# A recurrent attention block in front of a mixture of experts: the recurrence in halves of 64 steps, with matrix products of 64x64

## The chip, the core and the metric

The kernel runs on one core of one Trainium2 chip. Its time is the device time of one execution in microseconds (us); the time before is the median of three runs. A core has five engines that run their own instruction streams and wait for each other by semaphores: TensorE (PE in the profile, with its weight loads as PEld), VectorE (DVE), ScalarE (ACT), GpSimd (POOL) and SyncE (SP), which here issues most of the DMAs.

## What is computed

```python
# r, k, v: (4, 8, 768, 48); w, u: (8, 48); all fp32
for t in range(S):
    cur = np.einsum('bhd,bhe->bhde', u[None] * kt, vt)
    y[:, :, t] = np.einsum('bhd,bhde->bhe', rt, state + cur)
    state = w[None, :, :, None] * state + np.einsum('bhd,bhe->bhde', kt, vt)
# x: y as (3072 tokens, 384); then a mixture of experts, 4 groups of 4
g_idx = argmax(x @ w_group);  e_idx = argmax(x @ w_expert[g_idx])
out[token] = g_w * e_w * (relu(x @ w1[g, e]) @ w2[g, e])     # w1: 384x1024, w2: 1024x384
```

The gates `g_w` and `e_w` are the softmax values at the two chosen places. Each token goes to one expert of 16.

## The kernel before

**Tiles of the recurrence.** The 768 steps of each of the 4 sequences are cut into 6 chunks of 128. A tile `n` is one chunk of one sequence: `c = n // 4`, `b = n % 4`, 24 tiles, each with all 8 heads. Heads go in pairs: `hc` is the pair (4 of them), `e` the head in it, and a head is padded from 48 to 64 so that a pair fills 128 partitions. Decay is not applied step by step: r and k are scaled by powers of w (`T1T`, `T2`) that run over three chunks (`SPAN`), and the state is multiplied by the decay of the whole span (`w_span`) after each third chunk.

**One tile, in order.** `turn` transposes r and the scaled k of a tile on TensorE into two PSUM banks (`pr`, `pk`); VectorE scales `pr` into `rT`, ScalarE copies `pk` into `kT`. `scores` multiplies k and r of a tile, per head a product of 128 keys with 128 queries over 48 rows, into `pa0` and `pa1`; VectorE masks them by `later` into `am`. `values` adds the earlier state's share (`R`, one 128x128 product per pair, with zeros off the two diagonal blocks) and the products of `am` and v into one bank `py`; ScalarE copies it into `yT`. It then computes the update k times v into `pu`, and VectorE adds it to the state, for each half of the partitions on its own. `back` transposes `yT` into `pb`, and VectorE adds the step's own term `dv` into the token rows `xt`. `own` (GpSimd), `own_sum` (VectorE) and `own_values` (ScalarE, eight multiplications) make that term. `rows_T` transposes the rows again (`px`, copied by ScalarE to `xT`), and `row_logits` multiplies them by the gate weights into a bank `rb`.

**Routing.** After each four tiles the tokens are given to experts: `choice` (13 small VectorE operations and one exponential on ScalarE), `before` (two matrix products into a bank `pre`, which count the tokens ahead of each), `gate` and `place` (VectorE; `place` reads `pre`), and `rows`, an indirect DMA on GpSimd's queue that scatters the rows into `x_sorted`. `zero_places` fills the beginnings of the 16 regions of `x_sorted` with zeros, by DMAs on ScalarE's queue.

**The order** is written out by hand: every engine runs its instructions in the order of the program (line 103). The loop at line 691 goes over steps `s`: in step `s` the tile `s` is turned, `scores` runs for tile `s-1`, `values` for `s-2`, `back` for `s-3`, `rows_T` for `s-4`, `row_logits` for `s-5`. A step issues in this order: `before`; `turn`; GpSimd's scaling and `own`; `own_values`; `choice`; `rows_T`; `row_logits`; `back`; `values`; `own_sum`; `gate`, `place` and `rows`; `scores`. Choice runs in steps 9, 13, 17, 21 and 25, and `before`, `gate` and `place` in the step after each.

**Buffers.** PSUM has eight banks. Six form one set (line 82) that every user takes from as banks come free, and two are kept for routing (line 84). A bank is free again when its last reader has run. r and k are held in rings of four pairs of tiles, v in one of five. The weights of every second expert are later loaded into the memory of these rings.

**Experts.** From step 26 on the experts are computed, one item after another: `columns` (rows transposed into `px`), `up` (`ph`), `down` (`po`), `rows_out` (`pb`). The two largest experts' weights are loaded in steps 23 and 25, as soon as four chunks have been counted.

Of the kernel before, what the change touches and what calls it, by code (L numbers as in the profile page):

```python
# [30 lines left out]
RING = 4  # L31
# [3 lines left out]
def kernel(  # L35
# [29 lines left out]
    assert RING * 2 * H * D == KO * F and RING * 2 * H * DP >= FO * DM  # L65
# [16 lines left out]
    psum = ctx.enter_context(tc.tile_pool(name="psum", bufs=6, space=bass.MemoryType.PSUM))  # L82

    rpsum = ctx.enter_context(tc.tile_pool(name="rpsum", bufs=2, space=bass.MemoryType.PSUM))

    def bank(shape, name):
        return psum.tile(shape, FP32, tag="bank", name=name)
# [24 lines left out]


# [4 lines left out]
    khs = ring([P, 2, H, DP], "kh", RING - 1)  # L118
# [41 lines left out]

    first_use = cst([P, 1], "first_use")
# [16 lines left out]
    R = ring([P, HP, P], "R", B)  # L178
# [22 lines left out]
    for t in R:  # L201
        nc.gpsimd.memset(t, 0.0)
# [118 lines left out]
    def zero_places(j):  # L321

        regions = xs_dram.rearrange("(e n) w -> n e w", e=GE)
        part = CAP // 4
        nc.scalar.dma_start(out=regions[part * j : part * (j + 1)], in_=spread(nothing[0:part, :], 1, GE))
# [3 lines left out]
    def route_bank():  # L329

        return rpsum.tile([P, 512], FP32, tag="route", name="rb")

    def route(pool, rb, xt, T, sums, number, group):
# [28 lines left out]
        def choice():  # L362
            nc.vector.reduce_max(out=mx, in_=L, axis=AX)

            nc.vector.tensor_tensor(out=key, in0=L, in1=spread(mx, 3, Eg), op=OP.is_ge)
            nc.vector.tensor_mul(
                key.rearrange("p i a e -> p (i a) e"), key.rearrange("p i a e -> p (i a) e"), spread(desc, 1, T * NA)
            )
            nc.vector.reduce_max(out=kx, in_=key, axis=AX)
            nc.vector.tensor_tensor(out=ohg, in0=key[:, :, 0, :], in1=spread(kx[:, :, 0], 2, Eg), op=OP.is_equal)  # L370
            nc.vector.tensor_tensor(out=ohx, in0=key[:, :, 1:NA, :], in1=spread(kx[:, :, 1:NA], 3, Eg), op=OP.is_equal)
            nc.vector.tensor_mul(ohe, ohx, spread(ohg, 3, Eg))
            nc.vector.tensor_mul(ohp, ohx, spread(ohg, 3, Eg))
            for i in range(T):
                nc.vector.tensor_add(sums[:, i + 1, :], sums[:, i, :], ohp[:, i].rearrange("p g e -> p (g e)"))
            nc.vector.tensor_sub(ex, L, spread(mx, 3, Eg))
            nc.scalar.activation(ex, ex, AF.Exp)
# [30 lines left out]
        def rows(i):  # L408
# [8 lines left out]
        return choice, before, gate, place, rows  # L417
# [4 lines left out]
            kall.rearrange("p j a h d -> p (j a h d)").rearrange("p (k f) -> p k f", f=F),  # L422
# [53 lines left out]
    def columns(i):  # L476
        xg, w = xgs.pop(i), width(i)
        xe = xes[i] = item_tile(i, [P, KO, room(i)], "xe")
        for ks in (range(0, KO),) if KO * w <= 512 else (range(0, 2), range(2, KO)):
            px = bank([P, len(ks), w], "px")  # L480
            for q, ko in enumerate(ks):
                for j, n in enumerate(parts(i)):
                    nc.tensor.transpose(  # L483
                        px[:, q, P * j : P * j + n], xg[0:n, j, P * ko : P * (ko + 1)], ident[0:n, 0:n]
                    )
            nc.vector.tensor_copy(xe[:, ks[0] : ks[-1] + 1, 0:w], px)  # L486
        ids = item_tile(i, [P, 2], "ids", U32, bufs=4)
        gates = item_tile(i, [P, 2], "gates", bufs=4)
        for j, n in enumerate(parts(i)):
            nc.vector.tensor_scalar(  # L490
                out=ids[0:n, j : j + 1], in0=xg[0:n, j, DM + ROW_ID : DM + ROW_ID + 1], scalar1=float(N),
                scalar2=None, op0=OP.add,
            )
            nc.vector.tensor_copy(gates[0:n, j : j + 1], xg[0:n, j, DM + ROW_GATE : DM + ROW_GATE + 1])
        keys_of[i] = ids, gates

    def up(i, f):

        w = width(i)
        if f == 0:  # L500
            hTs[i] = item_tile(i, [P, FO, room(i)], "hT")
        w1, xe = weights[ITEMS[i][0]][0], xes[i]
        ph = bank([P, 2, w], "ph")
        for q in range(2):
            for ko in range(KO):
                nc.tensor.matmul(  # L506
                    ph[:, q, :], lhsT=w1[:, ko, P * (f + q) : P * (f + q + 1)], rhs=xe[:, ko, 0:w],
                    start=(ko == 0), stop=(ko == KO - 1), skip_group_check=True,
                )
        nc.scalar.activation(hTs[i][:, f : f + 2, 0:w], ph, AF.Relu)  # L510

    def down(i, d):

        w = width(i)
        if d == 0:
            yo[i] = item_tile(i, [P, KO, room(i)], "yo")
        w2, hT = weights[ITEMS[i][0]][1], hTs[i]
        po = bank([P, w], "po")
        for fo in range(FO):
            nc.tensor.matmul(  # L520
                po, lhsT=w2[:, fo, P * d : P * (d + 1)], rhs=hT[:, fo, 0:w], start=(fo == 0), stop=(fo == FO - 1)
            )
        nc.scalar.copy(yo[i][:, d, 0:w], po)  # L523

    def rows_out(i):
        y, (ids, gates) = yo.pop(i), keys_of.pop(i)
        for j, n in enumerate(parts(i)):
            pb = bank([P, DM], "pb")
# [17 lines left out]
    def scale_k(g, engine, a0=0, a1=2):  # L546
        m = g // (B // 2) % SPAN
        engine.tensor_mul(khs[g % (RING - 1)][:, a0:a1, :, 0:D], kts[g % RING][:, a0:a1], spread(T2[m], 1, a1 - a0))  # L548
# [20 lines left out]
    def turn(n):  # L569
# [3 lines left out]
        for dst, src in ((pr, rts[g % RING]), (pk, khs[g % (RING - 1)])):  # L573
# [7 lines left out]

    def scores(n):
        kT, rT = rkT[n]
        am = ams[n] = pool.tile([P, 2, HP, P], FP32, tag="am", bufs=2, name="am")
        pa = [bank([P, HP, P], f"pa{e}") for e in range(2)]
        for hc in range(HP):
            for e in range(2):
                rows = slice(DP * e, DP * e + D)
                nc.tensor.matmul(  # L589
                    pa[e][:, hc, :], lhsT=kT[rows, hc, :], rhs=rT[rows, hc, :],  # L590
                    start=True, stop=True, skip_group_check=True,
                )
        for e in range(2):
            nc.vector.tensor_mul(am[:, e], pa[e], spread(later, 1, HP))  # L594

    def values(n):
# [3 lines left out]
        vt, kh = vts[g % (RING + 1)], khs[g % (RING - 1)]  # L600
        rT, am = rkT.pop(n)[1], ams.pop(n)
        py = bank([P, HP, P], "py")
        if c > 0:
            for hc in range(HP):
                nc.tensor.matmul(
                    py[:, hc, :], lhsT=R[b][:, hc, :], rhs=rT[:, hc, :], start=(hc == 0), stop=False,
                    skip_group_check=True,
                )
        for hc in range(HP):
            for e in range(2):  # L610
                nc.tensor.matmul(  # L611
                    py[DP * e : DP * (e + 1), hc, :], lhsT=vt[:, a, 2 * hc + e, :], rhs=am[:, e, hc, :],
                    start=(c == 0), stop=True, skip_group_check=True,
                )
        yT = yTs[n] = pool.tile([P, HP, P], FP32, tag="yT", bufs=2, name="yT")
        nc.scalar.copy(yT, py)
        if c == NCH - 1:
            return
        pu = bank([P, HP, D], "pu")
        for hc in range(HP):  # L620
            for e in range(2):
                nc.tensor.matmul(
                    pu[DP * e : DP * (e + 1), hc, :], lhsT=kh[:, a, 2 * hc + e, :], rhs=vt[:, a, 2 * hc + e, 0:D],
                    start=True, stop=True, skip_group_check=True,
                )
        for e in range(2):
            rows = slice(DP * e, DP * (e + 1))
            state = R[b][rows, :, DP * e : DP * e + D]
            if c == 0:
                nc.vector.tensor_copy(state, pu[rows])  # L630
            elif c % SPAN < SPAN - 1:
                nc.vector.tensor_add(state, pu[rows], state)
            else:
                nc.vector.tensor_add(pu[rows], pu[rows], state)
                nc.vector.tensor_mul(state, pu[rows], spread(w_span[rows, :], 2, D))
# [55 lines left out]
    for s in range(NT + LAST):  # L691
# [11 lines left out]
        if s in (3, 5, 7, 9):  # L703
            zero_places(s // 2 - 1)
# [12 lines left out]
        if s < NT:  # L717
            turn(s)
            if s % 2 == 1 and s // 2 + 1 < NP:
# [3 lines left out]
        for n in range(NT):  # L723
            if s == max(n + 1, 2):
                own_values(n)
        run("choice")
# [7 lines left out]
        if 0 <= s - 2 < NT:  # L734
            values(s - 2)
# [3 lines left out]
        if 0 <= s - 1 < NT:  # L739
            scores(s - 1)  # L740
# [12 lines left out]
        if n in ROUTED:  # L753
            choice, before, gate, place, rows = routing(n)
            T = ROUTED[n]
            if n >= NT - B - 1:
                choice()
                todo.setdefault(s + 1, []).extend(
# [3 lines left out]
            else:  # L762
                todo.setdefault(s + 1, []).append(("choice", choice))
# [66 lines left out]
    with tc.If(more > 0, preferred_fallthrough_block=False):  # L830
        with tc.tile_pool(name="rest", bufs=1) as rest:
# [15 lines left out]
            with tc.If(ok < 1):  # L847
                with tc.tile_pool(name="scan", bufs=1) as sc:
# [54 lines left out]
                    with tc.For_i(0, NT, 1) as i:  # L903
# [10 lines left out]
                        for part in again[0:4]:  # L914
                            part()
                        again[4](0)
# [134 lines left out]
```

## Time and profile before

| what | value |
|---|---|
| runs | 480.11, 480.66 and 485.33 us; median 480.66 |
| the profiled execution | 479.58 us, of it 477.9 us from the first to the last instruction |
| mean granted TensorE clock | 0.973 |
| tile 8 is turned at | 52.6 us |
| tile 14 is turned at | 96.2 us |
| tile 23, the last, is turned at | 150.8 us |
| DMA share of the 16 engines, 28.3 to 96.2 us / 96.2 to 150.8 us | 1.16 / 0.32 |
| experts alone, 188 to 470 us: TensorE busy | 280.4 of 282 us |

The times of the tiles are the starts of the first transposes into `pr`. A share above 1 means that packets overlapped on their engines. TensorE's busy time is the union of its instructions' spans, ends modelled; it says that the engine had something in flight, not that it ran at its peak. In the lists below, a group's entry is the start, the time from its first start to its last end, the engine, the line, the operation, what it writes and reads, and how many instructions. An fp32 matrix product is two instructions, each with its own weight load; a transpose is one.

### The profile page before, as it was taken

To read this page: it belongs to the slowest core of one execution; us is meant where nothing else is said; L and a number is where in the kernel's file an instruction comes from. 1 tells how busy PE (TensorE), PEld (TensorE's weight loads), DVE (VectorE), ACT (ScalarE), POOL (GpSimd) and SP (SyncE) were. 2 spreads that over 40 slices of the span, in tenths; PEclk is the share of its full clock that TensorE was granted. 3 is DMA by queue.
4 is the path that set the end of the run, shared out by engine and by line. 5 is a ranking of instruction groups with operands and counts; after the bars stand their busy time and mean duration, and the time that the engine had idled before them with its cause. 6 is when DMAs were issued, how large, how long until landed. Compare 5 with 4: busy or idle time off the path is not lost. (4 is left out here: it accounts for less than half of the span.)

```text
span 477.9 us, 9090 instructions
## 1 busy us (share of the span) xinstructions
PE 449.7 (94%) x3623; PEld 430.6 (90%) x3623; DVE 159.5 (33%) x478; ACT 139.0 (29%) x418; POOL 129.5 (27%) x135
## 2 busy tenths in 40 slices
PE   3799999999999898999999999999999999999992
PEld 2598888899999798999999999999999999999991
DVE  5546566877778663010110210110110110111000
ACT  2846553564656321111121111111111111111120
POOL 7834536556564042000010210110120110120011
PEclk9969979999999989999999999999999999999997
DMA  9999999983102994565465754755856765666000
GB/s 176 187 190 228 207 227 202 200 155 77 36 35 69 339 335 132 188 239 168 160 190 182 256 184 153 280 201 156 284 190 198 255 188 199 238 202 236 30 22 26
DMA packets 112024, 86.24 MB, mean 180 GB/s; under 512 B 79633, under 2 KB 103568, under 8 KB 111976
## 3 DMA queue, kind: packets, MB, share of 16 engines
q1 hardware_dynamic: 98920, 68.81, 52.1%
q10 hardware_dynamic: 8432, 7.31, 7.1%
q0 software_dynamic: 4624, 9.48, 5.8%
q8 instruction: 30, 0.49, 0.5%
q14 instruction: 18, 0.15, 0.1%
HBM read 69.79 MB, written 16.12 MB: 180 GB/s over the span
## 5 line engine op out<-in xcount | busy, mean ns | idle before, releaser
L534 POOL DMA_INDIRECT out_dram<-yt,ids x32 | 34.1, 1066 | 255.0 <-DVE yt L532 250.4
L506 PE MATMUL ph<-xe,w 128*128 128x128 f32 (+7 forms) x432 | 72.2, 325 | 0.7 <-DVE xe L486 0.7
L520 PE MATMUL po<-hT,w 128*128 128x128 f32 (+7 forms) x432 | 71.4, 322 | 0.0
L506 PEld LDWEIGHTS ph<-xe,w 128*128 128x128 f32 x432 | 69.0, 194 | 1.2 <-DVE xe L486 0.9
L532 DVE TENSOR_SCALAR yt<-pb,gates 128x384 f32<-128x384 f32 (+15 forms) x32 | 18.3, 611 | 153.4 <-PE pb L530 153.4
L520 PE MATMUL po<-hT,rall 128*128 128x240 f32 (+7 forms) x384 | 68.6, 336 | 0.0
L506 PE MATMUL ph<-xe,kall 128*128 128x240 f32 (+7 forms) x384 | 68.4, 335 | 0.0
L520 PEld LDWEIGHTS po<-hT,w 128*128 128x128 f32 x432 | 67.8, 190 | 0.5
L510 ACT ACTIVATE hT<-ph 128x256 f32<-128x256 f32 (+15 forms) x68 | 33.5, 493 | 112.9 <-PE ph L506 112.9
L520 PEld LDWEIGHTS po<-hT,rall 128*128 128x128 f32 x384 | 65.0, 190 | 0.7
L506 PEld LDWEIGHTS ph<-xe,kall 128*128 128x128 f32 x384 | 64.9, 190 | 0.6
L523 ACT COPY yo<-po 128x128 f32<-128x128 f32 (+15 forms) x51 | 16.3, 320 | 127.7 <-PE po L520 127.7
L564 ACT ACTIVATE dv<-vt,du 128x48 f32<-128x48 f32 x192 | 45.8, 324 | 1.1 <-DVE du L558 1.0
L594 DVE TENSOR_TENSOR am<-pa,later 128x512 f32<-128x512 f32 x48 | 30.9, 685 | 9.0 <-PE pa L589 8.7
L486 DVE COPY xe<-px 128x384 f32<-128x384 f32 (+30 forms) x32 | 14.0, 475 | 53.6 <-PE px L483 53.6
L410 POOL DMA_INDIRECT x_sorted<-xt,place_i x24 | 23.8, 990 | 27.9 <-issue 14.0
L589 PE MATMUL pa<-rT,kT 48*128 48x128 f32 x384 | 29.3, 291 | 0.7 <-DVE xt L646 0.7
L611 PE MATMUL py<-am,vt 128*64 128x128 f32 x384 | 29.2, 290 | 0.7 <-DVE am L594 0.6
L553 POOL TENSOR_TENSOR dg<-rall,kall 128x768 f32<-128x768 f32 x12 | 21.9, 1821 | 28.9 <-DVE du L558 28.9
L548 POOL TENSOR_TENSOR kh<-kall,T 128x768 f32<-128x768 f32 (+1 forms) x12 | 21.4, 1788 | 28.0 <-DMA kall<-in_k_dram 9.7
L611 PEld LDWEIGHTS py<-am,vt 128*64 128x64 f32 x384 | 22.7, 143 | 4.7 <-DVE am L594 1.5
L589 PEld LDWEIGHTS pa<-rT,kT 48*128 48x128 f32 x384 | 24.4, 193 | 2.6 <-DVE xt L646 0.9
(128 smaller groups left out, 469.6 us busy)
## 6 DMA issues: line engine op xcount, KB each, us to landing
w<-in_moe_w_dram SPq DMA_DIRECT2D x16, 1536.0 KB, 6.8
kall<-in_moe_w_dram SPq DMA_DIRECT2D x8, 1536.0 KB, 7.1
rall<-in_moe_w_dram SPq DMA_DIRECT2D x8, 1536.0 KB, 6.8
x_sorted<-nothing ACTq DMA_DIRECT2D x4, 1544.0 KB, 10.2
rall<-in_r_dram SPq DMA_DIRECT2D x12, 384.0 KB, 7.2
vt<-in_v_dram SPq DMA_DIRECT2D x12, 384.0 KB, 6.8
kall<-in_k_dram SPq DMA_DIRECT2D x10, 384.0 KB, 6.4
xg<-x_sorted SPq DMA_DIRECT2D x17, 193.0 KB, 6.2
```

Source lines behind the costliest of these rows:

```text
L410: ins = nc.gpsimd.indirect_dma_start(out=xs_dram, out_offset=bass.IndirectOffsetOnAxis(ap=place_i[:, i : i + 1], axis=0), in_=xt[:, i, :], ...
L506: nc.tensor.matmul(ph[:, q, :], lhsT=w1[:, ko, P * (f + q) : P * (f + q + 1)], rhs=xe[:, ko, 0:w], start=(ko == 0), stop=(ko == KO - 1), s ...
L510: nc.scalar.activation(hTs[i][:, f : f + 2, 0:w], ph, AF.Relu)
L520: nc.tensor.matmul(po, lhsT=w2[:, fo, P * d : P * (d + 1)], rhs=hT[:, fo, 0:w], start=(fo == 0), stop=(fo == FO - 1))
L532: nc.vector.tensor_scalar(out=yt[0:n], in0=pb[0:n], scalar1=gates[0:n, j : j + 1], scalar2=None, op0=OP.mult)
L534: ins = nc.gpsimd.indirect_dma_start(out=out, out_offset=bass.IndirectOffsetOnAxis(ap=ids[0:n, j : j + 1], axis=0), in_=yt[0:n], in_offset ...
L548: engine.tensor_mul(khs[g % (RING - 1)][:, a0:a1, :, 0:D], kts[g % RING][:, a0:a1], spread(T2[m], 1, a1 - a0))
L553: nc.gpsimd.tensor_mul(dg, rts[g % RING][:, :, :, 0:D], kts[g % RING])
L564: nc.scalar.mul(dv[:, h, :], vts[g % (RING + 1)][:, a, h, 0:D], dvs[g][:, a, h : h + 1])
L589: nc.tensor.matmul(pa[e][:, hc, :], lhsT=kT[rows, hc, :], rhs=rT[rows, hc, :], start=True, stop=True, skip_group_check=True,)
L594: nc.vector.tensor_mul(am[:, e], pa[e], spread(later, 1, HP))
L611: nc.tensor.matmul(py[DP * e : DP * (e + 1), hc, :], lhsT=vt[:, a, 2 * hc + e, :], rhs=am[:, e, hc, :], start=(c == 0), stop=True, skip_gr ...
```

## The change

The 128 steps of a tile are split in two halves of 64 (`q`). There are now two states per tile, and the state is kept in three buffers per sequence, so that the state before a half is still there when it is read. `scores` and `values` compute only the two diagonal blocks of 64x64 for each head, and `update` one product per half and head; each product has 64 rows (48 in `scores`), 64 columns of weights and 64 (48 in `update`) moving columns, and in these three functions four in a row lie on four different quarters of the array. `from_state` multiplies each half's queries by the state before it: two blocks per pair of heads and half, on the two diagonal quarters, in place of one 128x128 product. The mask is 64 wide (`later_half`).

`update` now comes straight after `turn`, and `values` straight after `update`. `choice` moves from before `rows_T` to after `back`, its exponential to the end of the step, and `own_values` of tile 0 one step later. PSUM is cut into four sets of two banks: "bank" (`pr`, `pk`, `px`, `pb`, `pre` and small ones), "scores" (`pa` and `pu` share its two banks, by columns), "values" (`py0`, `py1`) and "route". The rings are one pair longer. The zero fill is eight DMAs, in steps 2 to 9, in place of four in steps 3, 5, 7 and 9. The experts keep their order; their tiles are given to these sets.

```diff
-RING = 4
+RING = 5
-    psum = ctx.enter_context(tc.tile_pool(name="psum", bufs=6, space=bass.MemoryType.PSUM))
-
-    rpsum = ctx.enter_context(tc.tile_pool(name="rpsum", bufs=2, space=bass.MemoryType.PSUM))
-
-    def bank(shape, name):
-        return psum.tile(shape, FP32, tag="bank", name=name)
+    psum = ctx.enter_context(tc.tile_pool(name="psum", bufs=2, space=bass.MemoryType.PSUM))
+
+    def bank(shape, name, tag="bank"):
+        return psum.tile(shape, FP32, tag=tag, name=name)
...
-        part = CAP // 4
+        part = CAP // 8
...
+    def update(n):
...
+        pu = [t[:, HP * HALF :].rearrange("p (c d) -> p c d", c=HP) for t in both]
+        halves = 2 if c < NCH - 1 else 1
+        for hc in range(HP):
+            for q in range(halves):
+                half = slice(HALF * q, HALF * (q + 1))
+                for e in range(2):
+                    nc.tensor.matmul(
+                        pu[q][DP * e : DP * (e + 1), hc, :], lhsT=kh[half, a, 2 * hc + e, :],
+                        rhs=vt[half, a, 2 * hc + e, 0:D], start=True, stop=True, skip_group_check=True,
+                    )
+        for q in range(halves):
+            old, new = state(n, q)[:, :, 0:D], state(n, q + 1)[:, :, 0:D]
+            if c == 0 and q == 0:
+                nc.vector.tensor_copy(new, pu[q])
+            elif q == 0 or c % SPAN < SPAN - 1:
+                nc.vector.tensor_add(new, pu[q], old)
+            else:
+                nc.vector.tensor_add(pu[q], pu[q], old)
+                nc.vector.tensor_mul(new, pu[q], spread(w_span, 2, D))
...
+    def from_state(n):
...
+        py = pys[n] = [bank([P, HP, HALF], f"py{q}", "values") for q in range(2)]
+        for q in range(2):
+            if c == 0 and q == 0:
+                continue
+            half = slice(HALF * q, HALF * (q + 1))
+            for hc in range(HP):
+                for e in range(2):
+                    rows = slice(DP * e, DP * (e + 1))
+                    nc.tensor.matmul(
+                        py[q][rows, hc, :], lhsT=state(n, q)[rows, hc, :], rhs=rT[rows, hc, half],
+                        start=(hc == 0), stop=False, skip_group_check=True,
+                    )
+
     def scores(n):
...
+        pa = [t[:, 0 : HP * HALF].rearrange("p (c t) -> p c t", c=HP) for t in both]
         for hc in range(HP):
             for e in range(2):
                 rows = slice(DP * e, DP * e + D)
-                nc.tensor.matmul(
-                    pa[e][:, hc, :], lhsT=kT[rows, hc, :], rhs=rT[rows, hc, :],
-                    start=True, stop=True, skip_group_check=True,
-                )
+                for q in range(2):
+                    half = slice(HALF * q, HALF * (q + 1))
+                    nc.tensor.matmul(
+                        pa[e][half, hc, :], lhsT=kT[rows, hc, half], rhs=rT[rows, hc, half],
+                        start=True, stop=True, skip_group_check=True,
+                    )
         for e in range(2):
-            nc.vector.tensor_mul(am[:, e], pa[e], spread(later, 1, HP))
+            nc.vector.tensor_mul(am[:, e], pa[e], spread(later_half, 1, HP))
...
+        if s <= NT:
+            both = [bank([P, HP * (HALF + D)], f"pa{e}", "scores") for e in range(2)]
+        if s < NT:
+            update(s)
+        if 0 <= s - 2 < NT:
+            values(s - 2)
...
-            if s == max(n + 1, 2):
+            if s == n + 2:
                 own_values(n)
-        run("choice")
...
         if 0 <= s - 3 < NT:
             back(s - 3)
-        if 0 <= s - 2 < NT:
-            values(s - 2)
+        run("choice")
...
         if 0 <= s - 1 < NT:
+            from_state(s - 1)
             scores(s - 1)
```

## The prediction

> **What bounds the kernel now.** I read the page first, then TensorE's waits, then the timeline of single steps.
>
> ```profile
> PE 449.7 (94%) x3623; PEld 430.6 (90%) x3623; DVE 159.5 (33%) x478; ACT 139.0 (29%) x418; POOL 129.5 (27%) x135
> ...
> PEclk9969979999999989999999999999999999999997
> DMA  9999999983102994565465754755856765666000
> ```
>
> TensorE has work in flight almost always. A slice is 12 us: the DMA engines are full for the first 98 us, and two early slices (24 to 36 and 60 to 72 us) run at a reduced clock. From 188 us on the experts fill TensorE (280.4 of 282 us) and the change leaves their products alone, so only the stretch before counts. It has two parts: tiles 8 to 14 took 43.6 us (52.6 to 96.2) under full DMA engines, tiles 14 to 22 took 48.9 us, two groups of four steps at 24.4. A step of the second part, TensorE alone:
>
> ```profile
> 108.40 0.66 PE L575 MATMUL pr<-ident,rall 128*128 128x128 f32 x4
> 108.89 0.60 PE L575 MATMUL pk<-ident,kh 128*128 128x128 f32 x4
> 109.33 0.49 PE L438 MATMUL px<-ident,xt 128*128 128x128 f32 x3
> 109.66 0.74 PE L443 MATMUL rb<-gw,xT 128*128 128x20 f32 x6
> 110.25 0.63 PE L645 MATMUL pb<-ident,yT 128*128 128x128 f32 x4
> 110.72 1.06 PE L605 MATMUL py<-rT,R 128*128 128x128 f32 x8
> 111.70 1.09 PE L611 MATMUL py<-am,vt 128*64 128x128 f32 x16
> 112.63 0.62 PE L622 MATMUL pu<-vt,kh 128*64 128x48 f32 x16
> 113.18 1.16 PE L589 MATMUL pa<-rT,kT 48*128 48x128 f32 x16
> ```
>
> No idle time is listed: the step is 5.87 us of matmul starts, of which the four recurrence groups are 0.98 + 0.93 + 0.55 + 1.09 = 3.55 (start to start; the next starts at 114.27). Three steps of 5.87 and one with 0.63 of `pre` make 18.24 + 6.0 = 24.2, the 24.4 measured. So TensorE's own work sets this part. TensorE's waits (waiting tile, releaser: us in total, times, longest), few as they are, show what could replace it:
>
> ```profile
> PE pb L645 <- ACT yT L616: 2.9, 1, 2.9
> PE pa L589 <- DVE xt L646: 0.7, 1, 0.7
> PE py L605 <- DVE at L404: 0.4, 1, 0.4
> ```
>
> `py` computes nothing from `at`, nor `pa` from `xt`. `at` is the reader of `pre`, `xt` of `pb`: TensorE waited for a PSUM bank, even with six in common.
>
> A step with `choice`, VectorE first:
>
> ```profile
> 116.84 0.23 DVE L363 TENSOR_REDUCE mx<-rb 128x20 f32<-128x80 f32 x1
> ...
> 119.52 0.23 DVE L376 TENSOR_TENSOR ex<-rb,mx 128x80 f32<-128x80 f32 x1
> 119.67 0.55 DVE L646 TENSOR_TENSOR xt<-pb,dv 128x384 f32<-128x384 f32 x1
> ```
>
> ```profile
> 115.94 1.91 ACT L564 ACTIVATE dv<-vt,du 128x48 f32<-128x48 f32 x8
> 119.79 0.27 ACT L377 ACTIVATE ex<-ex 128x80 f32<-128x80 f32 x1 [1.94 <-DVE ex L376]
> 119.97 0.46 ACT L439 COPY xT<-px 128x384 f32<-128x384 f32 x1
> ```
>
> `choice` holds VectorE 2.9 us (116.84 to 119.75), and `xT` stands behind 1.91 us of `dv`. Both cost nothing now, since six banks let TensorE run ahead.
>
> **What the Trainium skill says.** (1) "TensorE: Matmul & The Clock Gate", LDWEIGHTS: a weight load takes its columns over 1.2 GHz, 107 ns for 128 and 53 for 64. The trace agrees: starts in `rb` (128 columns, 20 moving) are 111 ns apart, pairs in `pu` (64 columns, two column tiles) 58.5. So `pu` is bound by weight loads, and not by the number of instructions. (2) The same page ("Wait — 56ns, not 53.3ns?") gives a floor of 25 ns from start to start. In pairs the trace has 7 ns, but no mean under 29 (58.5 over 2): four at once are not shown. (3) "TensorEngine Tiling (Array Packing)", Tiling Modes: 64x64 is four tiles that work in parallel; a change of mode drains the array. The trace: 205 ns from the last `py<-R` to the first `py<-am` instead of 111. (4) The first page, Part 1: after an idle window of about 3.4 us the clock is halved. Here 2.88 us of idling at 18.8 us is followed by 8 us at 0.50.
>
> **The change on TensorE.** Four tiles at 58.5 ns: 32 products' instructions are eight fours, 0.47 us, for each of `update`, `values` and `scores` (before 0.55, 0.93, 1.09). `from_state` has 32 instructions on two diagonal tiles: 16 pairs x 58.5 = 0.93. With three entries into another mode that these do not contain, at about 0.12, the recurrence is 2.34 + 0.36 = 2.7, not 3.55. The step falls to 5.0. Lower bound for a four: 58.5, the load of 64 columns. Upper: 117, two pairs in turn; then each group is 0.93 and the recurrence 4.1. I take 58.5, as nothing in (1) depends on the number of tiles.
>
> **On the others, per step.** `am` becomes 2 x 0.42 (from 0.69 at 512 elements and 0.35 at 192) instead of 1.29; the state's additions stay two of 0.35; a third-chunk step has three operations, not four. `yT` is two copies of about 0.36, +0.13. Zero fill: four more issues of 0.65 on ScalarE, ahead of `kT`, in steps that wait for loads anyway: nothing. The longer ring lets SP issue a pair two steps sooner; the engines are full until 98 us and no tile after 14 waits for data, so nothing after 14, and before it a gain of at most the stalls. Setup: fewer GpSimd fills (1.9 us of `R`), two small copies more; hidden behind the first loads. `own_values` of tile 0 one step later can take away the 2.88 us stall and some of its slow clock, up to 5 us at 20 to 33 us; I count nothing, since the loads for tiles 8 to 10 pace what follows (DMA full). Experts: same order, two banks each for `px`/`pb` and `po`, four for `ph`; a bank comes back after two `down`s of 1.8 us against a 0.32 us copy: nothing.
>
> **The new waits** come from "bank" having two members for five users. Follow four steps from the starts of `turn`; 0.25 us is a matmul's end plus the semaphore.
>
> Plain step: `update` writes the banks that the last step's `am` reads. `scores` ends at -0.1, `am` runs 0.3 to 1.15, `update` starts at 1.2 and not at 0.95: 5.25.
>
> `choice` step: pb starts at 3.2, `xt` runs 3.9 to 4.4, then `choice` to 7.3, then `am` to 8.15. The next `pre` needs `choice` and starts near 7.2 instead of 5.25, +2, and takes 0.62: 7.9.
>
> `pre` step: `pre` keeps one of two banks until `place`, at the end of the step; pr, pk, px and pb pass one by one through the other. pk waits for `rT`, which stands behind `am`: +1.0. `pb` waits for `xT`. ScalarE has `yT` at 3.3 to 4.0, `dv` to 5.9, `xT` to 6.4, so pb starts at 6.45 and not at 3.95: +2.5. Sum 5.0 + 3.5 = 8.5.
>
> The step after: `xt` ends at 7.7 of the step before, `own_sum` (0.95) at 8.65, `gate` (1.0), `place` (0.65) at 10.3, which is 1.8 into this step; pk, due at 0.5, waits 1.4, and `am` behind `place` holds `update` a little: 6.7.
>
> Four steps: 5.25 + 7.9 + 8.5 + 6.7 = 28.3 against 24.4, **+3.9**. `pre` falls on steps 10, 14, 18 and 22 with turns around them: four groups, +15.6. In tiles 8 to 14 the old kernel spent 43.6 us on 1.5 groups (36.6), so 7 us there were loads and slow clock; the new one's 42.5 fit beside these. That takes 7 off: **+9**. The weights of the first expert follow the count at step 22, and the experts follow them; all move by the same amount. Against the profiled execution, 479.6 + 9 = 488.6; the median of the runs is 1.1 above it. I say **489**.
>
> **Rivals.** (A) Likeliest, 0.55: the above. Its own range is 483 (half of the waits) to 498 (no relief from the loads). (B) Faster, 0.25: the bank waits do not bind, because VectorE and ScalarE get through a step sooner than laid out. It is decided by pk and pb of the `pre` steps and by `pre` behind `choice`: if these three lose less than 3.4 us in four steps (I have 2 + 3.5 + 1.4), TensorE's 0.85 us per step wins. With no wait, 10 steps after tile 14 give 8.5, the stalls before it up to 7: 464 to 472. Against: `py<-at` shows such waits with three times the banks. For: VectorE was 72% busy at 100 to 140 us (28.8 of 40), so there is some room. (C) 0.10: fours do not run at once. Then the recurrence is 4.1 us, and ten to fourteen steps lose 1.4 more than in (A), partly inside its waits: 495 to 508. (D) 0.10: waits and saving cancel, 475 to 484. A slow clock after waits of 2 us and more would add to (A) up to some 4 us a time, half of an 8 us stretch.
>
> **The numbers.** About 1% (4.8 us) is what a measurement here can tell from no change. Faster by more: (B), 0.25. Within: (D) and the lower edge of (A), 0.13. Slower: 0.62. The range 466 to 502 leaves out the best of (B) and the worst of (C).
>
> **What would show it.** Right: groups of 32 at 0.47 to 0.6 us; waits of pk for `rT` or `at`, of pb for `xT`, of `pre` for `choice`; steps of unequal length, 5 to 8.5. Wrong: even steps near 5.2 (B), groups of 32 at 0.9 (C), or experts longer than 282 us.

## The result, and the profile after

| | before | after |
|---|---|---|
| median of the runs | 481.19 us (4 runs, 480.11 to 485.33) | 526.43 us (4 runs, 522.89 to 528.91) |
| ratio, with 95% interval | 1 | 1.0931 [1.0846, 1.1016] |
| span of the profiled execution | 477.9 us | 527.2 us |
| mean granted TensorE clock in it | 0.973 | 0.899 |

The change makes the kernel 9.3% slower. The forecast was 489 us with a range to 502: the direction was right, the size was not, by a factor of five. The two spans differ by 49.3 us, and the starts of `turn` say where, beside what the prediction's own sum put there (one and a half groups of four at +3.9 less 7 for tiles up to 14, two and a half groups after it, nothing for the experts):

| stretch | before | after | difference | forecast |
|---|---|---|---|---|
| start to tile 4 | 28.3 | 27.1 | -1.2 | |
| tile 4 to tile 5 | 7.0 | 19.6 | +12.6 | |
| tile 5 to tile 14 | 60.9 | 68.5 | +7.6 | |
| together, to tile 14 | 96.2 | 115.2 | +19.0 | -1 |
| tile 14 to tile 23 | 54.6 | 73.5 | +18.9 | +10 |
| tile 23 to the end | 327.1 | 338.5 | +11.4 | 0 |

The page of the changed kernel, busy times and clock (a slice is 13.2 us here), and from its list of DMA queues the one that carries instructions (packets, MB, share of 16 engines):

```profile
PE 469.5 (89%) x5319; PEld 440.9 (84%) x5319; DVE 148.3 (28%) x478; ACT 141.6 (27%) x444; POOL 129.2 (25%) x145
...
PEclk9966896898969655599999999999999999999997
DMA  9999999660100059134654764746575647565300
...
q8 instruction: 43, 0.70, 0.6%
```

TensorE has 1696 matrix instructions more and is busy for a smaller share, but for 19.8 us longer (449.7 us before). The clock row, which had a 6, a 7 and an 8 ahead of the experts, now has eleven reduced digits up to 224 us, the last three of them 5, at 184 to 224 us. The queue of instructions moved 43 packets of 16 KB (before: 30).

A plain step of the changed kernel, TensorE's timeline (start, time to the last end, line, operation, tiles, count):

```profile
131.88 0.66 PE L582 MATMUL pr<-ident,rall 128*128 128x128 f32 x4
132.37 0.60 PE L582 MATMUL pk<-ident,kh 128*128 128x128 f32 x4
132.90 0.68 PE L605 MATMUL pa<-vt,kh 64*64 64x48 f32 x32
133.40 0.66 PE L667 MATMUL py<-am,vt 64*64 64x64 f32 x32
133.99 0.55 PE L445 MATMUL px<-ident,xt 128*128 128x128 f32 x3
134.38 0.74 PE L450 MATMUL rb<-gw,xT 128*128 128x20 f32 x6
134.97 0.63 PE L683 MATMUL pb<-ident,yT 128*128 128x128 f32 x4
135.53 1.08 PE L635 MATMUL py<-rT,R 64*64 64x64 f32 x29
...
136.51 0.64 PE L650 MATMUL pa<-rT,kT 48*64 48x64 f32 x30
```

The group at line 605 is `update`. From start to start it takes 0.50 us and `values` 0.59, for 32 instructions each: eight fours at 62 and 74 ns. The next `pr` starts at 137.07, so the step is 5.19 us where it was 5.87. The products do what the sum said. TensorE's waits in the first 240 us (waiting tile, releaser: us in total, times, longest) show what took the gain:

```profile
PE pb L683 <- ACT kT L586: 14.3, 2, 12.4
PE pa L650 <- issue: 7.6, 13, 3.4
...
PE pb L683 <- ACT xT L446: 5.0, 4, 1.5
PE pk L582 <- DVE rT L584: 3.5, 4, 0.9
...
PE pa L605 <- issue: 2.0, 1, 2.0
```

`xT` and `rT` are the bank waits that were forecast. The others were not: one wait of 12.4 us for a ScalarE copy, and two gaps of 3.4 and 2.0 us that the trace puts down to "issue", that is to nothing that it shows. (The other twelve of the 13 in the line of `pa L650` are 0.3 to 0.5 us long and lie in the steps of `choice` and after `pre`; experiment 3 comes back to them.)

**The 12.4 us.** ScalarE's own timeline there:

```profile
41.13 0.32 ACTq L330 DMA_DIRECT2D x_sorted<-nothing  x1
41.55 0.59 ACT L586 COPY kT<-pk 128x512 f32<-128x512 f32 x1 [12.42 <-DMA kall<-in_k_dram]
```

and SyncE's queue:

```profile
34.97 1.43 SPq L132 DMA_DIRECT2D kall<-in_k_dram  x1
```

The copy into `kT` waits for nothing of its own. It stands behind a DMA issue, a piece of the zero fill, which ran at 41.13, when the load of `kall` issued at 34.97 had landed. In the single record of that issue, the semaphore that it waits for is the one that it then raises itself, and the load of `kall` was the last to use it. The loads and the zero fill share a few semaphores in turn, so an issue can stand until an unrelated load has landed, with everything behind it on its engine. The Trainium skill, "DMA: Bandwidth & Descriptors", Anatomy of one DMA, a section on DMAs that GpSimd issues, says that any semaphore wait of a DMA happens on the issuing sequencer before dispatch. The trace agrees for this DMA of ScalarE's: it is ScalarE that stood, for 12.42 us. I call this theory Z.

ScalarE's timeline of the kernel before had the same sign, at the third of its four pieces:

```profile
49.97 0.60 ACTq L325 DMA_DIRECT2D x_sorted<-nothing  x1
50.67 0.58 ACT L579 COPY kT<-pk 128x512 f32<-128x512 f32 x1 [4.72 <-DMA vt<-in_v_dram]
```

`pk` had been written by 47.83, so the copy came some 2.8 us late. It cost nothing there: TensorE has no wait of over 0.3 us between 36 and 60 us. The prediction priced a piece by its issue alone, here 0.60 us, and not by what stands behind it until then.

**The gaps called issue.** TensorE's timeline inside one `scores` group:

```profile
78.94 0.40 PE L650 MATMUL pa<-rT,kT 48*64 48x64 f32 x10
82.72 0.91 PE L650 MATMUL pa<-rT,kT 48*64 48x64 f32 x20 [3.38 <-issue]
```

No wait stands between two products of one group, and yet TensorE paused for 3.38 us. In the records of the instruction queue a packet of 16 KB starts at 79.8 and ends at 81.2. The Trainium skill, "Runtime: NRT & Kernel Launch", Instruction fetch mechanics, says that each engine's instructions are refilled by DMA in blocks of 16 KiB, 256 instructions, and calls the cost "mostly hidden". The trace agrees with the size (0.70 MB in 43 packets; 13 packets more for 3392 TensorE instructions more, 261 each) and, in this place, not with the hiding. With its weight loads a step had 154 TensorE instructions and now has 298, so 256 last 4.5 us (256/298 of 5.19) and not 9.8, while the DMA engines are full until 92 us. Theory I: instructions arrive late.

**The bank waits.** The start of the `pre` step that begins at 145.1 us:

```profile
145.12 1.06 PE L582 MATMUL pr<-ident,rall 128*128 128x128 f32 x4
147.05 1.09 PE L582 MATMUL pk<-ident,kh 128*128 128x128 f32 x4 [0.88 <-DVE rT L584]
148.07 1.11 PE L605 MATMUL pa<-vt,kh 64*64 64x48 f32 x32
```

pk waits for `rT`, as laid out, and later pb for `xT`. But each group also takes nearly twice its time in the plain step (1.11 against 0.68): the granted clock is at half, from 144.2 to 151.0 us.

**The tail.** Windows of the trace (start, end, length; busy us of PE, PEld, DVE, ACT, POOL; granted clock; DMA share; GB/s):

```profile
168.00:176.00 8.00, 6.97 (x139) 6.06 (x137) 5.32 (x20) 3.67 (x13) 5.45 (x4) 0.93 0.15 53
176.00:184.00 8.00, 6.09 (x67) 5.16 (x66) 1.05 (x2) 3.49 (x13) 0.00 (x0) 0.50 0.00 0
184.00:192.00 8.00, 7.28 (x108) 6.36 (x107) 5.25 (x19) 0.00 (x0) 2.85 (x3) 0.50 0.23 52
...
200.00:208.00 8.00, 7.47 (x131) 6.79 (x123) 1.31 (x3) 2.81 (x11) 0.00 (x0) 0.50 1.01 366
```

The clock is at half from 174.9 us, at the start of the last `pre` step, to 222.7 us, well into the experts, whose products are the same as before.

### The profile page after: what moved, and what is told of

Its sections match the earlier page's. It is cut to its first block, busy times and chain, and to the rows that moved or that the text cites. A ratio compares the mean times of both kernels' runs of the same rounds, so it can differ in the third digit from the quotient of the medians.

```text
span 527.2 us, 12511 instructions
## 1 busy us (share of the span) xinstructions
PE 469.5 (89%) x5319; PEld 440.9 (84%) x5319; DVE 148.3 (28%) x478; ACT 141.6 (27%) x444; POOL 129.2 (25%) x145
## 5 line engine op out<-in xcount | busy, mean ns | idle before, releaser
L527 PEld LDWEIGHTS po<-hT,w 128*128 128x128 f32 x432 | 67.8, 190 | 0.5
L683 PE MATMUL pb<-ident,yT 128*128 128x128 f32 x96 | 18.6, 326 | 19.3 <-ACT kT L586 14.3
L417 POOL DMA_INDIRECT x_sorted<-xt,place_i x24 | 23.8, 991 | 48.9 <-issue 23.1
L586 ACT COPY kT<-pk 128x512 f32<-128x512 f32 x24 | 14.0, 585 | 76.5 <-PE pk L582 48.8
L650 PE MATMUL pa<-rT,kT 48*64 48x64 f32 x768 | 27.3, 261 | 7.6 <-issue 7.6
L635 PE MATMUL py<-rT,R 64*64 64x64 f32 x704 | 30.9, 248 | 0.5 <-ACT yT L673 0.5
L635 PEld LDWEIGHTS py<-rT,R 64*64 64x64 f32 x704 | 27.2, 158 | 4.8 <-issue 3.2
L683 PEld LDWEIGHTS pb<-ident,yT 128*128 128x128 f32 x96 | 14.0, 182 | 20.1 <-ACT kT L586 14.7
L684 DVE TENSOR_TENSOR xt<-pb,dv 128x384 f32<-128x384 f32 x24 | 13.4, 558 | 61.2 <-PE pb L683 56.7
```

What stands on the lines that cost most here:

```text
L417: ins = nc.gpsimd.indirect_dma_start(out=xs_dram, out_offset=bass.IndirectOffsetOnAxis(ap=place_i[:, i : i + 1], axis=0), in_=xt[:, i, :], ...
L527: nc.tensor.matmul(po, lhsT=w2[:, fo, P * d : P * (d + 1)], rhs=hT[:, fo, 0:w], start=(fo == 0), stop=(fo == FO - 1))
L635: nc.tensor.matmul(py[q][rows, hc, :], lhsT=state(n, q)[rows, hc, :], rhs=rT[rows, hc, half], start=(hc == 0), stop=False, skip_group_chec ...
L650: nc.tensor.matmul(pa[e][half, hc, :], lhsT=kT[rows, hc, half], rhs=rT[rows, hc, half], start=True, stop=True, skip_group_check=True,)
L683: nc.tensor.transpose(pb[:, hc].rearrange("p e d -> p (e d)"), yT[:, hc, :], ident)
```

## The experiments

Each ratio is to the kernel before, run beside it (medians 480.61 us for 1 to 4, 478.95 for 5 to 8, 479.62 for 9 to 12); "after" is the changed kernel, 526.43 us. Where no number of runs is given it is two. Times within a kernel are from its one profiled execution.

**1. The zero fill alone.** The changed kernel with the four pieces of before.

```diff
-        part = CAP // 8
+        part = CAP // 4
-        if 2 <= s < 10:
-            zero_places(s - 2)
+        if s in (3, 5, 7, 9):
+            zero_places(s // 2 - 1)
```

> The changed kernel with the zero fill of before: four pieces in steps 3, 5, 7 and 9. Theory Z (a piece in an even step follows the three loads of that step in the program and has to wait on ScalarE, ahead of kT, for the landing of an earlier load whose semaphore it takes over): the step from tile 4 to tile 5 falls from 19.6 us to 6 to 8, the 12.4 us wait of pb for kT is gone, and the time falls by 12 to 18 us, to 508 to 514. Rival (the stall comes from the loads themselves, or from banks): the stall stays, time within 3 us of 526.

Measured: 507.13 us, ratio 1.0599 [1.039, 1.0808], 19.3 below after, just under the range expected. Tile 4 to tile 5 takes 8.9 us and not 19.6, a little more than expected; of the 14.3 us behind `kT`, 1.8 are left. The gaps called issue grew: 2.5, 2.7 and 3.5 us ahead of 70 us. So the zero fill made the longest single wait, and something else takes a part of what the edit gives back: tile 14 comes only 8.6 us sooner. Another 6.3 us come back from there to tile 23, and 7.4 after it, with less half clock (the mean is 0.939, after 0.899).

**2. `place` ahead of `gate`.** `place` reads `pre` first in the step, so that its bank comes back early.

```diff
-    [("first", before), ("last", gate), ("last", place)]
+    [("first", before), ("first", place), ("last", gate)]
```

> The changed kernel with place straight after before, so that the bank of pre comes free at the start of its step. Theory B (pre keeps one of two banks for a whole step): the waits of pk for rT and of pb for xT (0.9 and 1.0 to 1.5 us, four of each) vanish, the pre steps fall from 10 to 10.6 us to 6.5 to 7.5 and the steps after them from 6.7 to about 5.3, and with less slow clock the time falls by 14 to 25 us. Rival (the slow clock alone makes these steps long, or VectorE's lateness): pre steps stay above 9 us, time falls by less than 5 us.

Measured: 497.90 us, ratio 1.0407 [1.0156, 1.0657], 28.5 below after, more than expected. The waits in the same stretch:

```profile
PE pb L683 <- ACT kT L586: 12.6, 2, 12.2
...
PE pre L388 <- DVE rb L378: 4.0, 4, 1.0
...
PE pk L582 <- DVE at L411: 1.1, 3, 0.4
```

Nothing is left of pb behind `xT` (5.0) and of pk behind `rT` (3.5): the bank that `pre` held was the cause of both. `pre` behind `choice` now shows by its name (`rb` is of `choice`), as it does in experiment 1. The `pre` steps take 5.7 to 6.8 us where they took 10.0 to 13.0. That is more than the 8.5 us of waits, and windows from tile 14 to tile 23, of after and of this run, say why:

```profile
115.16:188.71 73.55, 63.63 (x1306) 55.63 (x1305) 36.38 (x110) 31.40 (x113) 28.66 (x21) 0.79 0.09 30
113.81:168.93 55.12, 49.81 (x1305) 44.10 (x1305) 35.57 (x108) 31.67 (x114) 28.01 (x19) 1.00 0.13 39
```

The same products kept TensorE busy for 63.6 us at a mean clock of 0.79 and for 49.8 at full clock. Of the 18.4 us between the stretches, 13.8 are this and 4.6 idle time. The clock is higher at 176 to 222 us too (0.89), and from tile 23 on it takes 328.9 us and not 338.5.

**3. `choice` back before `rows_T`.**

```diff
+        run("choice")
         if 0 <= s - 4 < NT:
             rows_T(s - 4)
...
             back(s - 3)
-        run("choice")
```

> The changed kernel with choice back in its old place, ahead of rows_T, the exponential left at the end of the step. Theory C (choice behind back ends so late that am and pre wait): the choice steps fall from 8.0 us to about 6, four or five of them, 8 to 12 us in all. Rival (what VectorE does is only moved: xt and with it own_sum and am then stand behind choice): choice steps fall by less than 0.7 us, time within 4 us of 526.

Measured: 504.07 us, ratio 1.0535 [1.0317, 1.0754], 22.4 below after, where 8 to 12 were expected. After tile 9 the `choice` steps fall from 7.7 to 8.0 us to 5.7 to 5.9, as laid out, and the small gaps called issue in them are gone. In after, `pre` starts as soon as `choice` has written `cum` (written by 144.15 us, `pre` at 144.21), so I read those gaps as the wait of `pre` for `choice`, come early. `pre` steps stay long, 8.3 to 10.4. The shortest of them, tile 14, ran at full clock throughout:

```profile
112.11:120.44 8.33, 5.56 (x149) 4.79 (x150) 3.38 (x8) 3.49 (x13) 2.21 (x2) 1.00 0.40 95
```

From tile 23 on it is 327.2 us. Again more came back than the waits that the edit takes away.

**4. All three.**

> All three edits at once. If Z, B and C are right and independent: 526 - 14 - 18 - 9, about 485, with plain steps of 5.2 us, no step of tiles 8 to 23 above 7 us and a mean clock of 0.95 or more. If the loss lies in the products of 64x64 or in the halves themselves, it stays above 505.

Measured: two runs, 485.83 and 493.68 us, too far apart for a ratio; about 485 was expected. The profile is of the longer one, a span of 491.9, 35.3 below after. The three gains sum to 70 us and give 33 to 41 together. One part of the overlap is shown: each of the edits alone brings back 7 to 11 us after tile 23, where only 11.4 were lost. From tile 14 on steps are now even (plain 5.2, `choice` 5.7 to 5.9, `pre` 5.6 to 6.5), and tiles 14 to 22 take 45.3 us, less than the 48.9 of before. But the step of tile 9 takes 13.8 us, where none above 7 was expected, and tile 8 is turned at 63.6 us, where before had 52.6: in this execution one zero fill piece still waits for a load (5.9 us), and three gaps called issue make 8.2 us.

**5. The eight pieces in the kernel before.** If Z is right, the old kernel must pay for them too; if the longer ring is to blame, it must not.

```diff
-        part = CAP // 4
+        part = CAP // 8
-        if s in (3, 5, 7, 9):
-            zero_places(s // 2 - 1)
+        if 2 <= s < 10:
+            zero_places(s - 2)
```

> The kernel before with the zero fill of the change alone: eight pieces, steps 2 to 9. Theory Z (a piece issued on ScalarE right behind a step's loads takes over the semaphore of a load that has not landed, and holds kT and all that follows on ScalarE): a stall of 5 to 15 us in the first 60 us, TensorE waiting for ScalarE, time 487 to 497. Rival (the piece stalls only because the longer ring lets SP run ahead): time within 3 us of 481.

Measured: 486.37 us (483.56 and 489.19), ratio 1.0155 [1.0031, 1.0279], some 7 us more and just under the range expected. ScalarE's timeline in the shorter run:

```profile
36.54 0.32 ACTq L325 DMA_DIRECT2D x_sorted<-nothing  x1
36.96 0.59 ACT L579 COPY kT<-pk 128x512 f32<-128x512 f32 x1 [7.22 <-DMA vt<-in_v_dram]
```

The same picture with another load: ScalarE stands for 7.22 us, and at 36.4 us TensorE has a wait of 3.3 us for ScalarE that the kernel before does not have. (Another, of 3.5 us at 19.5, has its like there, 2.9 us at 18.8.) The step from tile 5 to tile 6 takes 11.1 us and not 5.0. Z holds without the longer ring.

**6. The pieces on SyncE's queue**, with the three edits of experiment 4.

```diff
-        nc.scalar.dma_start(out=regions[part * j : part * (j + 1)], in_=spread(nothing[0:part, :], 1, GE))
+        nc.sync.dma_start(out=regions[part * j : part * (j + 1)], in_=spread(nothing[0:part, :], 1, GE))
```

> The three edits (zero fill in four pieces in steps 3, 5, 7, 9; place right after before; choice ahead of rows_T), and the zero fill issued by SP in place of ScalarE. Theory Z: the remaining 5.9 us wait of pb for kT goes, 486 to 490 becomes 478 to 483. If the loads pace these steps anyway, or the waits for instructions grow in its place: within 3 us of 488.

Measured: 490.70 us (3 runs), ratio 1.0247 [1.0165, 1.033]; no gain. The wait for `kT` is gone, and this stands in its place (first 160 us):

```profile
PE py L635 <- issue: 6.5, 2, 3.5
...
PE py L667 <- issue: 4.9, 1, 4.9
PE pr L582 <- issue: 4.2, 1, 4.2
...
PE pa L650 <- issue: 1.8, 1, 1.8
```

17.4 us, and tile 14 is turned at 106.7 us, in experiment 4 at 107.2. I read this so: the wait had covered gaps that come anyway as soon as TensorE runs faster through its instructions. My main expectation failed here; the branch for theory I was met.

**7. The ring of four**, with the three edits.

```diff
-RING = 5
+RING = 4
```

> The three edits with the rings at their old length. If the longer ring does harm (SP runs ahead, takes up all semaphores and keeps the DMA engines full), the early steps shorten: tile 8 is turned 4 to 8 us sooner than at 63.6. If it helps, tile 8 comes later. If loads pace the early steps either way: within 3 us.

Measured: 486.09 us (18 runs, 479.11 to 493.24), ratio 1.0117 [1.0087, 1.0148]. The profiled execution was the fastest of them: tile 8 at 57.0 us (experiment 4: 63.6), and still gaps of 2.2, 1.6, 1.9 and 2.9 us. The gaps remain. Whether the shorter ring brings the early tiles sooner is not shown, since here the fastest execution stands against the slower one of experiment 4.

**8. and 9. Only more instructions.** To measure theory I by itself, the kernel before, with the products of `scores` and of `am` with v cut into more instructions, meant to take the same array time: twice as many (218 per step) in 8, four times (346) in 9. Nothing else changes. The edit of 9 in `scores`:

```diff
+                for q in range(4):
+                    part = slice(32 * q, 32 * (q + 1))
                     nc.tensor.matmul(
-                        pa[e][:, hc, :], lhsT=kT[rows, hc, :], rhs=rT[rows, hc, :],
+                        pa[e][part, hc, :], lhsT=kT[rows, hc, part], rhs=rT[rows, hc, :],
...
```

> The kernel before with the same products cut into twice as many instructions at the same array time: scores with 64 columns of weights in place of 128 (two per head), values with 64 moving columns in place of 128; 64 more instructions per step counting weight loads, none left out. Theory I (the gaps that the profile calls issue, 2 to 3.5 us, each beside the landing of a 16 KB instruction fetch while the DMA engines are full, come from TensorE using up its instructions faster): the kernel before, which has none, gets one to three such gaps before 100 us and 3 to 8 us. Rival (they belong to 64x64 tiles or to the new order): none appears, time within 3 us of 481.

> The kernel before with scores and values cut into four times as many instructions at the same array time (32 columns of weights, tiles of 64x32 and 128x32): 346 TensorE instructions in a step with weight loads, 256 of them (16 KB) in about 4.4 us, as fast as the changed kernel takes them (298 in 5.2 us); twice as many, in 6.9 us, brought no gap. Theory I (a fetch under full DMA engines takes some 4 to 5 us from when it is asked for, and TensorE runs dry when it uses up 16 KB sooner): gaps called issue of 1 to 4 us appear before 100 us, two to five of them, and 4 to 12 us are lost. Rival (the gaps belong to the 64x64 tiles or the new order): none, within 3 us of 479.

Measured: 479.23 us for 8 (18 runs), ratio 1.0023 [0.9995, 1.0052], with no gap called issue: a miss. At 5.87 us a step, 256 instructions last 6.9 us there, and that is long enough. For 9 it is 496.75 us, ratio 1.0382 [1.0322, 1.0441]; 256 instructions last some 4.4 us. Its waits and a piece of its TensorE timeline:

```profile
PE pa L591 <- issue: 8.0, 4, 3.4
PE py L617 <- issue: 6.1, 3, 3.0
```

```profile
48.05 0.62 PE L591 MATMUL pa<-rT,kT 48*32 48x128 f32 x19
52.12 1.29 PE L591 MATMUL pa<-rT,kT 48*32 48x128 f32 x37 [3.44 <-issue]
```

The old kernel, with its old buffers and order, has the gaps once its instructions run out as fast as in the new one. They make some 14 of the 17 us; a plain step is also about 0.2 us longer. From 97 to 166 us, at a DMA share of 0.35, the same instructions go without any gap called issue, so it is not their shape that pauses. The instruction queue fits too: in after and the experiments there are 26 gaps called issue of over 1.2 us in the first 240 us; each ends 1.3 to 1.8 us after a packet of 16 KB on that queue has landed, and in each the DMA share, taken from 2 us ahead of the gap, is 0.84 to 1.21. Theory I stands.

**10. The change without the halves.** Whole 128-step products, one state, in the new order, bank sets, ring and zero fill.

```diff
+    WHOLE = 24
     def scores(n):
+        if n < WHOLE:
+            for hc in range(HP):
+                for e in range(2):
+                    rows = slice(DP * e, DP * e + D)
+                    nc.tensor.matmul(
+                        pa[e][:, hc, :], lhsT=kT[rows, hc, :], rhs=rT[rows, hc, :],
+                        start=True, stop=True, skip_group_check=True,
+                    )
...
+            return
```

> The change without its halves: whole tiles of 128 steps as before (one update, one state, full scores and values), all else of the change kept: four sets of two banks, order, longer rings, zero fill in eight. If order, banks and zero fill carry the loss: 515 to 535, with the stall of tile 4 to 5, choice steps near 8.5 us and pre steps of 10. If the halves carry it: under 500.

Measured: 522.28 us, ratio 1.0915 [1.0793, 1.1038], within the error of after. Steps are 6.16 (plain), 7.59 (`choice`), 9.7 to 13.3 (`pre`), and up to 6.95 after `pre`. So the rest of the change alone costs as much as the whole, and the halves' saving is used up: without them no gap called issue is left in the first 240 us and the mean clock is 0.960, with them it is 0.899.

**11. Without halves, with the three edits and the ring of four.**

> Whole tiles as in the run before, with the three edits and the short rings: 476 to 484, no gap called issue over 1 us, steps near 6 us.

Measured: 486.55 us, ratio 1.0169 [1.0109, 1.0228], a little above what was expected, with no gap called issue. Tiles 14 to 22 take 52.1 us, two groups of four at 26.1, 1.6 a group more than before. The two-member bank sets and what is left of the new order cost that together; no run here parts them.

**12. Whole products for the first 12 tiles, halves for the rest**, with the three edits and the ring of four: few instructions while the DMA engines are full, small products after it.

> The three edits and the short rings, whole tiles for the first 12, while the DMA engines are full, halves for the other 12. If theory I is right and the halves pay where instructions come in time: tile 12 turned at about 82 us as before, then steps of 5.7 us on average in place of 6.1, 472 to 477, faster than both. If halves bring nothing even there: 479 or more.

Measured: 480.40 us (20 runs), ratio 1.0022 [0.9992, 1.0052]: no difference from before, and a miss by 3 us and more. Tiles 12 to 23 take 64.6 us where before has 67.8; tile 12 is turned 1.7 us later, and from tile 23 on it takes 328.7 us, 1.6 more. The time alone would fit the rival, that halves bring nothing here; by the steps the gain is there and is given back on both sides. A group of four in halves (tiles 14 to 18) is 22.4 us against 26.1 in experiment 11, so halves are worth 0.9 us a step. No version tried beats the kernel before.

## Why the prediction was right in kind and wrong in size

**TensorE's sum was right.** 2.7 us were forecast for the recurrence and a plain step of 5.0 to 5.25; the step is 5.19. Fours at once hold, so (C) falls. Experiments 11 and 12 give 0.9 us a step between whole and halved tiles, where the sum had 0.85.

**Three of the four new waits were right as mechanisms.** `choice` steps were forecast at 7.9 and are 7.7 to 8.0 after tile 9. pk behind `rT`, pb behind `xT` and `pre` behind `choice` are in the traces, and experiments 2 and 3 take them away by moving `place` and `choice`. A `pre` step was forecast at 8.5, and the one at full clock (experiment 3) took 8.33. (B) falls as well: its 3.4 us in four steps are exceeded.

**One was right by luck.** The steps after `pre` were forecast at 6.7 and are 6.1 to 6.8, but the 1.4 us of pk behind `place` are not in the trace: in the step of tile 15, pk follows pr at once (125.16 and 126.07 us, at half clock). The half clock at its start makes it some 0.9 us longer than the plain step, and a gap called issue in `pa` some 0.6.

**The failed steps, in the order of the sum:**

1. "Zero fill: four more issues of 0.65 on ScalarE, ahead of `kT`, in steps that wait for loads anyway: nothing." I priced the issue's duration and not what the issue itself may wait for. It cost 12.4 us in one place and 1.9 in another; experiment 1 returns 19 us, 8.6 of them before tile 14, and experiment 5 finds some 7 us in the old kernel. The "cover", loads that TensorE waits for anyway, was thinner than the wait.

2. "That takes 7 off." The relief of tiles 8 to 14 assumed that faster steps would fit beside the loads. To tile 14 the kernel lost 19.0 us, and all of it is idle time of TensorE, by the windows of before and after:

```profile
0.00:96.16 96.16, 82.14 (x920) 74.76 (x920) 59.75 (x150) 49.68 (x164) 53.31 (x71) 0.91 1.14 202
0.00:115.16 115.16, 82.15 (x1864) 72.20 (x1864) 54.82 (x154) 49.60 (x170) 54.89 (x82) 0.85 1.00 185
```

The two stalls behind `kT` make 14.3 us, and late instructions 2.0 and 3.4. TensorE's busy time did not fall, at a mean clock of 0.85 and not 0.91. The doubling of the instruction count was in my working only as array time; "bound by weight loads, and not by the number of instructions" is right about the array and says nothing of the fetch. Experiment 9 shows that late instructions alone can cost some 14 us.

3. The `pre` step: "Sum 5.0 + 3.5 = 8.5." The three `pre` steps after tile 14 took 10.0, 10.6 and 13.0, 8.1 us above this, which is nearly all of the excess in that stretch (18.9 against 10). The waits themselves, 0.9 and 1.0 to 1.5 us, are no longer than forecast (1.0 and 2.5); the groups between them ran at half the clock, for 4.9, 7.2 and all of the 13.0 us. Experiment 2 measures what that costs from tile 14 to tile 23: 13.8 us. I had set the slow clock beside the sum ("would add to (A) up to some 4 us a time"), not in it, and only for waits of 2 us and more. The 8 us that I took from the trace of before were short as well: the clock there was at half from 22.3 to 32.6 us.

4. "the experts follow them; all move by the same amount." They moved by 11.4 us more, since the half clock lasted 48 us, 34 of them after tile 23. Any one of the first three edits brings back at least 7 of the 11.4, so waits before tile 23 feed it. I tried no kernel that changes the clock alone, so which wait starts it stays open. So does the rule by which the semaphores are handed out, and why the trace calls the wait of `pre` for `choice` issue in after.

So the terms of steps 1 and 2 make 20 us of the 40 between forecast and result. The other 20, 9 up to tile 23 and 11 after it, are the half clock: in the first of these stretches its 13.8 us are more than the excess, and in the second, where nearly all products are those of before, the clock is at half for 34 us ahead of the end, and for 3.4 in the kernel before. The range to 502 left out both, since I bounded only those costs that I had priced. A small slip besides: 488.6 and the 1.1 us to the median make 489.7, not 489.

## What to carry to other kernels

A DMA issued from a compute engine's queue is a place where that engine can stand until some earlier transfer has landed (12.4 us here), so ask what its semaphore was used for last and what stands behind it, and not how long the issue takes. A buffer that is held across a step shrinks its set for every other user: move its reader to the front of the step (one line gave 28 us here, more of it through the clock than through the waits). So price a series of short waits with the slow clock in the sum. Smaller products mean more instructions, and while loads fill the DMA engines, the stream of instructions is itself a transfer that can be late (here where 256 of them lasted 4.5 us).

## What was not expected of the hardware

- Four 64x64 products on four quarters of the array do run at once: 32 instructions in 0.50 us from start to start, about 62 ns for four.
- TensorE can pause for 1.3 to 4.9 us, often inside a group, with no semaphore, where 256 of its instructions are used up in about 4.4 us and the DMA engines are full; at 6.9 us per 256 it never did. The new instructions' packet took 1.4 us in the case shown, and the first product came 1.5 us after it had landed.
- The clock stayed at half for 48 us, although TensorE had work in flight for 76 to 93% of the windows shown at 0.50, and no wait in the 30 us before it was longer than 1.5 us, well under the 3.4 us of the idle window in the prediction's place (4). Here the measurement goes beyond what that place explains.
- In the clock records of after, every stretch at half ahead of that one is 3.4 us long or a multiple of it (17.1, 3.4, 13.7, 3.4, 3.4, 6.8, 3.4), so here none lasted less than 3.4 us, whatever started it.
